# The product of w3 and w_out made in three chunks of 256 columns in place of two of 384

## The chip, the cores and the metric

One Trainium2 chip, one core. The metric is device time in microseconds of one execution. A difference is read from repeated runs of both kernels, taken side by side.

## What is computed

Attention over 4 batches of 12 heads with a soft cap, then four matrix products in a row on 1792 tokens:

```python
scores = cap * np.tanh(scale * q @ k.T / cap)
attn = softmax(scores)
x = (attn @ v)                      # laid out as 1792 x 768
a = x @ w1                          # 768 x 1024
b = x @ w2                          # 768 x 1024
h = a * b @ w3                      # w3: 1024 x 1024
out = h @ w_out                     # w_out: 1024 x 768
```

Weights are given as float64 and are split on the chip.

## The kernel before

The last two products are not made in the order of the reference. With u = a * b, the kernel makes C = w3 x w_out first (1024 x 768, it depends on no token) and then out = u x C. The second product is made by a scheme of Strassen's kind: seven products of quarter matrices, whose right operands are quarters of C and their differences.

The operands of these products are held as a high and a low part in fp32r. A product is three matmuls: high x high, high x low, low x high. Weights come as 64-bit floats: a *piece* of up to 384 columns is loaded as pairs of 32-bit words and turned into a high and a low part by a row of VectorE steps (lines 234, 246, 251, 254, 264, 271) and one or two ScalarE steps (239, and 268, the cast of the high part, which VectorE may also take).

The order on each engine is written out when the program is built, by a planner (`Plan.run`). Each step is a task with an engine (or two engines to choose from), a cost in ns, a key, and the tasks that it needs. The planner always takes the engine that is free first, and for it the ready task with the smallest key. What it emits is the fixed order of each engine's queue; on the chip each engine goes through its queue in that order, and waits on semaphores.

The stage that is changed is `plan_C(n)`, for n = 0 to 7. Each n makes one block of 128 rows of C: `it = ITS[n]` takes the rows in the order 0, 4, 1, 5, ..., so an upper block (`lower` = 0) is followed by the lower block with the same k. Before the change each n has two halves, nh = 0 and 1, of NH = 384 columns:

- 8 PE tasks (jt = 0 to 7, of three matmuls each, line 981) accumulate into one PSUM bank of the pool `ps_f`, which has six. The left operand is the w3 block (`w3t`, tile `w3x`, two buffers), the right one the rows `wo[jt]` of w_out. The three w3 pieces of a block cover jt = 0 to 2, 3 to 5 and 6 to 7 (`JG`). A task costs 521 in the plan. Its key is K0 + 40 + (n * 2 + nh) * 8 + jt.
- One copy (line 1006, task `D`) takes the bank to SBUF as `c`, 128 x 384, on ScalarE or VectorE, key K0.
- Then `split` makes the high part (line 1025, ScalarE or VectorE) and the low part (line 1029, VectorE) of that block, and `combine` (line 1050, VectorE) the differences; their keys, K0 - 1, come before those of the w3 pieces (K0 + 11.5 and up). The upper block gives B11 and T1, the lower one B21, B22, T2, T3 and T4.

After it come the output tasks (`plan_out`, line 1175, keys K0 + 200 and up): for each of seven t the seven products in the order 1, 5, 2, 3, 6, 7, 4, with 12 matmuls of 384 columns each. The first takes B11, the second T1, the third B21. The loads of `A` (line 1083) are issued on SP's queue, as the loads of the w3 pieces (line 227) are.

Of the kernel before, what the change touches and what calls it, by code (L numbers as in the profile page):

```python
# [8 lines left out]
F32 = mybir.dt.float32  # L9
# [139 lines left out]
def program(  # L149
# [16 lines left out]
    nc = tc.nc  # L166
    P = 128
    B, H, S, D = 4, 12, 448, 64
    NT, DM = out.shape
# [4 lines left out]
    KF = DF // P  # L174
    NH = DM // 2
    PC = 384
    KM = 384
    QO = 4
    CP, NCH = 112, 4
    SH = S // 2  # L180
# [23 lines left out]
    plan = Plan()  # L204
    plan.wait = {"PE": 32, "ACT": 119, "DVE": 91, "POOL": 0, "SP": 0}
    done, use = {}, {}

    def put(name, eng, ns, key, emit, needs=(), lat=0.0, alt=(), after=()):
        done[name] = plan.add(
            eng, ns, key, emit, [done.get(x) for x in needs], lat, alt, [done[x] for x in after]  # L210
        )
        done[name].name = name
        return done[name]
# [102 lines left out]
    KQ = 2 * S  # L316
    HK = KQ if general else S + KM
    att = ExitStack()
# [36 lines left out]
    def cuts(pr):  # L355

        return [slice(0, S + P), slice(S + P, HK)] if pr == 0 else [slice(0, HK)]

    def plan_load(pr):
        key = due(pr, 0) if pr % 2 else due(pr, 1)  # L360

        def emit():
            raw_t[pr] = qkp.tile([P, QO + KQ], F32, tag="raw", name=f"kq{pr}", bufs=3)
            for c in cuts(pr):
                c = slice(c.start + QO if c.start else 0, (c.stop if c.stop < HK else KQ) + QO)
                nc.sync.dma_start(raw_t[pr][:, c], kq[pr][:, c])
# [12 lines left out]
    def plan_split(pr):  # L379
# [3 lines left out]
        for n, c in enumerate(cuts(pr)):  # L383
            w = (c.stop - c.start) / HK

            def high(copy, n=n, c=c):
                if n == 0:
                    hl_t[pr] = qkp.tile([P, 2, HK], F32R, tag="hl", name=f"hl{pr}")
                copy(hl_t[pr][:, 0, c], raw_t[pr][:, QO + c.start : QO + c.stop])  # L389

            def low(c=c):
                h, l = (hl_t[pr][:, i, c] for i in range(2))
                nc.vector.tensor_tensor(
                    l, raw_t[pr][:, QO + c.start : QO + c.stop], h, op=ALU.subtract
                )
# [17 lines left out]
    def quarter(pr, j):  # L413

        j ^= pr % 2
        return slice(j * D, (j + 1) * D)

    def plan_S(pr, i):
# [5 lines left out]
        def scores():  # L424
            box[0] = ps_s.tile([P, 2, 512], F32, tag="s", name=f"s{pr}_{i}")
            if i == 0:
                for n in range(2):
                    for j in range(2):
                        at = slice(j * D, (j + 1) * D)
                        nc.tensor.matmul(  # L430
                            box[0][quarter(pr + n, j), n, :S],
                            lhsT=raw_t[pr + n][at, QO + S + KM :],
                            rhs=raw_t[pr + n][at, QO : QO + S],
                            start=True,
# [268 lines left out]
    def plan_general(pr):  # L703
# [3 lines left out]
        def emit():  # L707
# [4 lines left out]
            for c in range(NCH):  # L712
# [25 lines left out]
                for j in range(2):  # L738
# [5 lines left out]
                    for m, k1 in enumerate(ends):  # L744
                        k0 = m * P if m < 3 else KM - at.start
                        nc.tensor.transpose(
# [137 lines left out]
    NRAW, NRT, NOB, NF = 6, 3, 9, 6  # L884
    K0, CK = 500, 0.72
# [80 lines left out]
    bt, cf = {}, {}  # L966

    def plan_C(n):

        it = ITS[n]  # L970
        k, lower = it % HF, it // HF
        for nh in range(2):
            ns = slice(nh * NH, (nh + 1) * NH)
            box = {}
            for jt in range(KF):

                def emit(jt=jt, box=box, nh=nh, ns=ns):
                    if jt == 0:
                        box[0] = ps_f.tile([P, 512], F32, tag="f", name=f"pc{it}_{nh}")
                    for z, (a, c) in enumerate(((0, 0), (0, 1), (1, 0))):  # L980
                        nc.tensor.matmul(  # L981
                            box[0][:, :NH],
                            lhsT=w3t[n % 2][:, a, jt, :],
                            rhs=wo[jt][:, c, ns],
                            start=(jt == 0 and z == 0),
                            stop=(jt == KF - 1 and z == 2),
                        )

                key = K0 + 40 + (n * 2 + nh) * KF + jt
                z = [i for i, x in enumerate(JG) if x[0] <= jt < x[1]][0]  # L990
                t = put(
                    f"C{n}_{nh}_{jt}", "PE", 521, key, emit,
                    [f"O{jt}_{nh}high", f"O{jt}_{nh}out", f"Z{n}_{z}high", f"Z{n}_{z}out"]
                    + [f"C{n}_{nh}_{jt - 1}"],
                )
                if jt == 0:
                    f = plan.tag("f", NF).take(t)
                use["wo", jt // 2].append(t)
                for u in (use["w3t", n], use["w3y"]):
                    u.append(t)  # L1000

            c = f"c{lower}{nh}_{k}"

            def evac(cp, box=box, c=c):
                cf[c] = obp.tile([P, NH], F32, tag="ob", name=c)
                cp(cf[c], box[0][:, :NH])

            t = put(
                f"D{c}", "ACT", 400, K0, lambda f=evac: f(nc.scalar.copy), [f"C{n}_{nh}_{KF - 1}"],
                0, [("DVE", 450, lambda f=evac: f(nc.vector.tensor_copy))],  # L1010
            )
            f.append(t)
            t.key = key
            use[c] = plan.tag("ob", NOB).take(t)
            t.key = K0
            use[c].append(t)

        def split(name, c, after):


            def high(copy):
                if not bt:
                    for x in RHS.values():
                        bt[x] = big.tile([P, HF, 2, NH], F32R, tag="W", name=f"b{x}")
                copy(bt[name][:, k, 0], cf[c])

            def low():
                h, l = (bt[name][:, k, x] for x in range(2))
                nc.vector.tensor_tensor(l, cf[c], h, op=ALU.subtract)

            first = (name, k) == ("B11", 0)
            t = put(
                f"h{name}_{k}", "ACT", 412, K0 - 1, lambda: high(nc.scalar.copy),
                [after] + ["hB11_0"] * (not first), 0,
                [("DVE", 269, lambda: high(nc.vector.tensor_copy))],
            )
            use[c].append(t)
            if first:
                t.key = key
                for x in RHS.values():  # L1040
                    plan.tag("W", KF).take(t)
                t.key = K0 - 1
            t = put(f"l{name}_{k}", "DVE", 470, K0 - 1, low, [f"h{name}_{k}"])
            use[c].append(t)

        def combine(name, to, a, b, needs):


            def emit():
                nc.vector.tensor_tensor(cf[to], cf[a], cf[b], op=ALU.subtract)  # L1050

            t = put(name, "DVE", 470, K0 - 1, emit, needs)
            for x in {to, a, b}:
                use[x].append(t)

        c11, c12, c21, c22 = (f"c{x}_{k}" for x in ("00", "01", "10", "11"))
        if not lower:
            split("B11", c11, f"D{c11}")
            combine(f"T1_{k}", c11, c12, c11, [f"D{c12}", f"lB11_{k}"])
            split("T1", c11, f"T1_{k}")  # L1060
        else:
            split("B21", c21, f"D{c21}")
            split("B22", c22, f"D{c22}")
            combine(f"T3_{k}", c12, c22, c12, [f"D{c22}", f"T1_{k}"])
            combine(f"T2_{k}", c11, c22, c11, [f"D{c22}", f"lT1_{k}"])
            split("T2", c11, f"T2_{k}")
            split("T3", c12, f"T3_{k}")
            combine(f"T4_{k}", c21, c11, c21, [f"T2_{k}", f"lB21_{k}"])
            split("T4", c21, f"T4_{k}")
# [184 lines left out]
    with tc.manual_schedule():  # L1254
# [52 lines left out]
        ps_f = fin.enter_context(tc.tile_pool(name="ps_f", bufs=NF, space=PSUM))  # L1307
        wop = fin.enter_context(tc.tile_pool(name="wop", bufs=1))
        obp = fin.enter_context(tc.tile_pool(name="obp", bufs=NOB))
# [6 lines left out]
        for n in range(KF):  # L1316
            for z in range(len(JG)):
                plan_w3(n, z)
            plan_C(n)
# [75 lines left out]
```

## Time and profile before

| | us |
|---|---|
| median of 3 runs | 591.85 |
| lowest and highest | 590.34, 593.38 |
| span of the profiled execution | 589.8 |
| TensorE matmul busy | 571.9 (97%) |
| TensorE weight load busy | 448.6 (76%) |
| VectorE busy | 424.2 (72%) |
| ScalarE busy | 320.8 (54%) |

The span is the time from the first to the last instruction of one profiled execution; its own time outside the profile is not recorded, and the median of the runs is 2.05 us above the span. Busy time of matmuls is taken from modelled ends and overlaps from one matmul to the next, so the spacing of matmuls has to be worked out from a stretch and a count, not from the length of one. The page names instructions by the line of the program, the engine and the tiles: `pc<-wo,w3x` is the product that is changed, `pab` the products with w1 and w2 before it, `m` the output products after it, `c` the copied block, `bB` and `bT` its splits. In the rows PE is TensorE's matmul, PEld its weight load, DVE is VectorE and ACT ScalarE.

### The profile page before, as it was taken

How to read it: one execution, taken by the hardware profiler on the slowest of the kernel's cores; microseconds unless marked ns; L12 is line 12 of the kernel's file. 1: busy time of each engine (PE TensorE's matmuls, PEld its weight loads, DVE VectorE, ACT ScalarE, POOL GpSimd, SP SyncE). 2: the span in 40 equal slices, each digit the busy share in tenths (PEclk: the TensorE clock that was granted, in tenths of full speed). 3: DMA queues.
4: the chain of work that ended last, by engine and by line, in shares of the span. 5: the costliest groups of instructions: out<-in, count | busy, mean ns of one | idle time of the engine just before them, and what ended most of it. 6: DMA issues, size and time to landing. Idle time of an engine off the chain costs nothing.

```text
span 589.8 us, 8978 instructions
## 1 busy us (share of the span) xinstructions
PE 571.9 (97%) x3324; PEld 448.6 (76%) x3324; DVE 424.2 (72%) x910; ACT 320.8 (54%) x478; POOL 0.2 (0%) x4
## 2 busy tenths in 40 slices
PE   6989899999999999999999999999999999999995
PEld 3334386665588676667767779999999999999995
DVE  5999999899963536451726135999999998876611
ACT  7989857588833654645636412444455563443300
POOL 0000000000000000000000000000000000000000
PEclk9999999999999999999999999999999999999999
DMA  7355645554620303141212006555432225444111
GB/s 255 97 155 172 200 148 182 170 166 138 211 69 33 126 20 130 40 127 32 81 47 64 32 33 208 188 181 168 153 117 98 89 82 161 135 155 140 55 54 59
DMA packets 46517, 70.35 MB, mean 119 GB/s; under 512 B 5890, under 2 KB 34178, under 8 KB 46466
## 3 DMA queue, kind: packets, MB, share of 16 engines
q1 hardware_dynamic: 46466, 69.71, 37.2%
q8 instruction: 28, 0.46, 0.3%
q14 instruction: 23, 0.19, 0.1%
HBM read 56.67 MB, written 12.93 MB: 118 GB/s over the span
## 4 chain that ended last, share of the span: by engine, by line
PE 80%; DVE 12%; DMA 3%; ACT 2%; issue 1%; SPq 1%; DVEq 0%; ACTq 0%
PE pab L832 39%; PE m L1175 17%; PE pv L496 7%; PE pc L981 7%; PE s L443 6%; DMA raw_w<-in_moe_w_dram 2%; PE sum L573 2%; DVE t_w L246 1%; PE pv L511 1%; DVE raw_w L254 1%; PE s L430 1%; DVE a L559 1%; ACT p L456 1%; DVE raw_w L251 1%; DVE w3x L271 1%
## 5 line engine op out<-in xcount | busy, mean ns | idle before, releaser
L832 PE MATMUL pab<-x,w_hl 128*128 128x448 f32 x1152 | 248.7, 371 | 0.0
L832 PEld LDWEIGHTS pab<-x,w_hl 128*128 128x128 f32 x1152 | 212.6, 188 | 39.0 <-issue 11.0
L459 ACT ACTIVATE p<-p,ncap_sb,acap_sb 128x896 f32<-128x896 f32 x84 | 92.4, 1138 | 0.0
L456 ACT ACTIVATE p<-s,tsc_sb 128x896 f32<-128x896 f32 x84 | 81.5, 1012 | 18.3 <-PE s L443 16.5
L981 PE MATMUL pc<-wo,w3x 128*128 128x384 f32 x384 | 67.1, 335 | 1.1 <-DVE w3x L271 1.1
L981 PEld LDWEIGHTS pc<-wo,w3x 128*128 128x128 f32 x384 | 66.5, 188 | 1.6 <-DVE w3x L271 1.4
L443 PE MATMUL s<-hl 64*128 64x448 f32 x432 | 59.5, 397 | 7.2 <-ACT hl L389 4.4
L443 PEld LDWEIGHTS s<-hl 64*128 64x128 f32 x432 | 37.6, 190 | 35.3 <-issue 13.4
L496 PE MATMUL pv<-p,v 128*64 128x448 f32 x288 | 62.7, 554 | 1.2 <-DMA v<-in_v_dram 0.9
L559 DVE TENSOR_TENSOR a<-p,p 128x896 f32<-128x896 f32 x24 | 26.1, 1086 | 47.0 <-ACT xf L633 33.5
L1175 PE MATMUL m<-bB,lx 128*128 128x384 f32 x252 | 45.9, 334 | 0.0
L1175 PEld LDWEIGHTS m<-bB,lx 128*128 128x128 f32 x252 | 43.9, 188 | 0.0
L496 PEld LDWEIGHTS pv<-p,v 128*64 128x64 f32 x288 | 17.5, 137 | 31.8 <-issue 23.3
L239 ACT ACTIVATE t_w<-t_w,rebias 128x384 int32<-128x384 int32 (+1 forms) x48 | 28.4, 597 | 23.5 <-DVE t_w L234 23.2
L633 ACT COPY xf<-pv 128x448 f32<-128x448 f32 x24 | 12.8, 535 | 36.7 <-PE pv L496 18.4
L857 DVE TENSOR_TENSOR u<-pab,u 128x448 f32<-128x448 f32 x32 | 19.6, 613 | 18.3 <-PE pab L832 18.1
L1125 ACT CAST lx<-A 128x512 fp32r<-128x512 f32 x32 | 19.4, 620 | 23.7 <-DVE A L1101 9.2
L1175 PE MATMUL m<-bT,lx 128*128 128x384 f32 x168 | 31.4, 334 | 0.0
L246 DVE SCALAR_TENSOR_TENSOR t_w<-raw_w,t_w 128x384 int32<-128x384 int32 (+1 forms) x56 | 29.8, 534 | 2.0 <-ACT t_w L239 1.7
L1175 PE MATMUL m<-bT,lw 128*128 128x384 f32 x168 | 30.2, 334 | 0.0
L254 DVE SCALAR_TENSOR_TENSOR raw_w<-raw_w 128x384 f32<-128x384 uint32 (+1 forms) x56 | 29.8, 532 | 0.2
L1175 PEld LDWEIGHTS m<-bT,lx 128*128 128x128 f32 x168 | 29.3, 188 | 0.0
(81 smaller groups left out, 567.3 us busy)
## 6 DMA issues: line engine op xcount, KB each, us to landing
raw_w<-in_moe_w_dram SPq DMA_DIRECT2D x48, 384.0 KB
kq<-in_kq_dram SPq DMA_DIRECT2D x23, 450.0 KB
u_dr<-u SPq DMA_DIRECT2D x32, 224.0 KB
A<-u_dr SPq DMA_DIRECT2D x28, 256.0 KB
raw_wo<-in_moe_w_out_dram SPq DMA_DIRECT2D x16, 384.0 KB
v<-in_v_dram SPq DMA_DIRECT2D x24, 224.0 KB
r<-r_dr SPq DMA_DIRECT2D x48, 112.0 KB
out_dram<-o SPq DMA_DIRECT2D x14, 192.0 KB
```

The costliest lines, as they stand in the source:

```text
L239: nc.scalar.activation(self.t, self.t, AF.Relu, bias=rebias, scale=4096.0)
L246: nc.vector.scalar_tensor_tensor(self.t, self.hi, SIGN, self.t, op0=ALU.bitwise_and, op1=ALU.bitwise_or)
L254: nc.vector.scalar_tensor_tensor(self.lo.bitcast(F32), self.lo.bitcast(U32), 2.0**-32, self.hi, op0=ALU.mult, op1=ALU.add,)
L443: nc.tensor.matmul(box[0][:, j, :S], lhsT=hl[at, a, S + (i - 1) * P : S + i * P], rhs=hl[at, c, :S], start=(z == 0), stop=(z == 2),)
L456: nc.scalar.activation(p, box[0][:, :, :S], AF.Tanh, scale=tsc_sb)
L459: nc.scalar.activation(p_t[pr, i], p_t[pr, i], AF.Exp, scale=acap_sb, bias=ncap_sb)
L496: nc.tensor.matmul(pv_t[pr][j * D : (j + 1) * D, :S], lhsT=v_t[pr][:, 3 * j + i - 1, :], rhs=p_t[pr, i][:, j, :], start=(i == 1 and not od ...
L559: nc.vector.tensor_tensor(a_t[pr], p_t[pr, 1], p_t[pr, 2], op=ALU.add)
L832: nc.tensor.matmul(box[0][:, :S], lhsT=w_t[m][:, a, wi, kt, :], rhs=x_t[b][:, c, kt, :], start=(kt == 0 and z == 0), stop=(kt == KX - 1 an ...
L857: nc.vector.tensor_tensor(box[2][0], box[1][0][:, :S], box[2][0], op=ALU.mult)
L981: nc.tensor.matmul(box[0][:, :NH], lhsT=w3t[n % 2][:, a, jt, :], rhs=wo[jt][:, c, ns], start=(jt == 0 and z == 0), stop=(jt == KF - 1 and ...
L1175: nc.tensor.matmul(box[banks[m]][:, :NH], lhsT=hl[g][:, i, a, k, :], rhs=bt[RHS[m]][:, k, c, :], start=(new and k == 0 and z == 0), stop=( ...
```

## The change

Each block of C is made in three chunks of CW = 256 columns, and not in two halves of 384. A chunk is eight PE tasks of three matmuls of 256 columns into one bank. The first chunk lies in the first half of the output columns, the third in the second; the second chunk lies in both, so it is copied by two tasks of 128 columns, one into each half's tile `c`. The splits and differences still work on the 384 columns of a half and need both of its copies. The planned cost of a PE task goes from 521 to 333, that of a copy is set by its width, and the keys of the PE tasks are spread over the same stretch as before.

```diff
@@ -175,6 +175,7 @@
     NH = DM // 2
     PC = 384
     KM = 384
+    CW = 256
     QO = 4
     CP, NCH = 112, 4
     SH = S // 2
@@ -969,29 +970,30 @@
 
         it = ITS[n]
         k, lower = it % HF, it // HF
-        for nh in range(2):
-            ns = slice(nh * NH, (nh + 1) * NH)
+        for ch in range(DM // CW):
+            ns = slice(ch * CW, (ch + 1) * CW)
+            halves = range(ns.start // NH, (ns.stop - 1) // NH + 1)
             box = {}
             for jt in range(KF):
 
-                def emit(jt=jt, box=box, nh=nh, ns=ns):
+                def emit(jt=jt, box=box, ch=ch, ns=ns):
                     if jt == 0:
-                        box[0] = ps_f.tile([P, 512], F32, tag="f", name=f"pc{it}_{nh}")
+                        box[0] = ps_f.tile([P, 512], F32, tag="f", name=f"pc{it}_{ch}")
                     for z, (a, c) in enumerate(((0, 0), (0, 1), (1, 0))):
                         nc.tensor.matmul(
-                            box[0][:, :NH],
+                            box[0][:, :CW],
                             lhsT=w3t[n % 2][:, a, jt, :],
                             rhs=wo[jt][:, c, ns],
                             start=(jt == 0 and z == 0),
                             stop=(jt == KF - 1 and z == 2),
                         )
 
-                key = K0 + 40 + (n * 2 + nh) * KF + jt
+                key = K0 + 40 + n * 2 * KF + (ch * KF + jt) * CW / NH
                 z = [i for i, x in enumerate(JG) if x[0] <= jt < x[1]][0]
                 t = put(
-                    f"C{n}_{nh}_{jt}", "PE", 521, key, emit,
-                    [f"O{jt}_{nh}high", f"O{jt}_{nh}out", f"Z{n}_{z}high", f"Z{n}_{z}out"]
-                    + [f"C{n}_{nh}_{jt - 1}"],
+                    f"C{n}_{ch}_{jt}", "PE", 333, key, emit,
+                    [f"O{jt}_{nh}{x}" for nh in halves for x in ("high", "out")]
+                    + [f"Z{n}_{z}high", f"Z{n}_{z}out", f"C{n}_{ch}_{jt - 1}"],
                 )
                 if jt == 0:
                     f = plan.tag("f", NF).take(t)
@@ -999,21 +1001,29 @@
                 for u in (use["w3t", n], use["w3y"]):
                     u.append(t)
 
-            c = f"c{lower}{nh}_{k}"
-
-            def evac(cp, box=box, c=c):
-                cf[c] = obp.tile([P, NH], F32, tag="ob", name=c)
-                cp(cf[c], box[0][:, :NH])
-
-            t = put(
-                f"D{c}", "ACT", 400, K0, lambda f=evac: f(nc.scalar.copy), [f"C{n}_{nh}_{KF - 1}"],
-                0, [("DVE", 450, lambda f=evac: f(nc.vector.tensor_copy))],
-            )
-            f.append(t)
-            t.key = key
-            use[c] = plan.tag("ob", NOB).take(t)
-            t.key = K0
-            use[c].append(t)
+            for nh in halves:
+                c = f"c{lower}{nh}_{k}"
+                a, b = max(ns.start, nh * NH), min(ns.stop, (nh + 1) * NH)
+                first = a == nh * NH
+
+                def evac(cp, box=box, c=c, a=a, b=b, nh=nh, first=first, at=ns.start):
+                    if first:
+                        cf[c] = obp.tile([P, NH], F32, tag="ob", name=c)
+                    cp(cf[c][:, a - nh * NH : b - nh * NH], box[0][:, a - at : b - at])
+
+                w = (b - a) / NH
+                t = put(
+                    f"D{c}" if b == (nh + 1) * NH else f"D{c}a", "ACT", 140 + 260 * w, K0,
+                    lambda f=evac: f(nc.scalar.copy),
+                    [f"C{n}_{ch}_{KF - 1}"] + [f"D{c}a"] * (not first),
+                    0, [("DVE", 60 + 390 * w, lambda f=evac: f(nc.vector.tensor_copy))],
+                )
+                f.append(t)
+                if first:
+                    t.key = key
+                    use[c] = plan.tag("ob", NOB).take(t)
+                    t.key = K0
+                use[c].append(t)
 
         def split(name, c, after):
```

## Rows read from the trace of the kernel before

**Rows 1.** The page: span, busy (share, instructions), clock, chain, `pab` group.

```profile
span 589.8 us, 8978 instructions
...
PE 571.9 (97%) x3324; PEld 448.6 (76%) x3324; DVE 424.2 (72%) x910; ACT 320.8 (54%) x478; POOL 0.2 (0%) x4
...
PEclk9999999999999999999999999999999999999999
...
PE 80%; DVE 12%; DMA 3%; ACT 2%; issue 1%; SPq 1%; DVEq 0%; ACTq 0%
...
L832 PE MATMUL pab<-x,w_hl 128*128 128x448 f32 x1152 | 248.7, 371 | 0.0
```

**Rows 2.** Chain that ended last, in order of time: start, length, what.

```profile
399.85 13.64 PE pab L832 x66
413.49 24.81 PE pc L981 x143
438.30 0.02 issue
438.32 0.42 DVE w3x L271
438.74 0.47 DVE c L1006
...
467.49 0.48 DVE w3x L271
467.97 0.04 issue
468.01 13.58 PE pc L981 x76
481.59 101.94 PE m L1175 x588
```

**Rows 3.** Instructions in order of time: start, length, what, idle before.

```profile
413.33 12.99 PE L981 MATMUL pc<-wo,w3x 128*128 128x384 f32 x74
...
468.01 13.27 PEld L981 LDWEIGHTS pc<-wo,w3x 128*128 128x128 f32 x76 [1.44 <-DVE w3x L271]
468.01 13.58 PE L981 MATMUL pc<-wo,w3x 128*128 128x384 f32 x76 [1.12 <-DVE w3x L271]
...
481.43 2.24 PE L1175 MATMUL m<-bB,lx 128*128 128x384 f32 x12
```

**Rows 4.** Waits of TensorE's matmuls from 400 us: total, times, longest.

```profile
PE pc L981 <- DVE w3x L271: 1.1, 1, 1.1
```

**Rows 5.** Windows: length, busy us of each engine (instructions), clock, DMA.

```profile
438.30:468.00 29.70, 28.59 (x165) 28.27 (x164) 29.67 (x81) 16.23 (x33) 0.00 (x0) 1.00 0.32 102
...
490.00:500.00 10.00, 10.00 (x60) 10.00 (x59) 8.22 (x15) 3.00 (x6) 0.00 (x0) 1.00 0.63 190
```

**Rows 6.** Chain in order of time, an earlier stretch of `pab`.

```profile
166.63 17.21 PE pab L832 x84
```

**Rows 7.** In order of time: two weight loads after the stall, second's matmul.

```profile
468.01 0.19 PEld L981 LDWEIGHTS pc<-wo,w3x 128*128 128x128 f32 x1 [1.44 <-DVE w3x L271]
...
468.12 0.19 PEld L981 LDWEIGHTS pc<-wo,w3x 128*128 128x128 f32 x1
...
468.29 0.52 PE L981 MATMUL pc<-wo,w3x 128*128 128x384 f32 x2
```

**Rows 8.** In order of time: copies of the sixth block's two halves.

```profile
461.84 0.46 ACT L1006 COPY c<-pc 128x384 f32<-128x384 f32 x1
...
463.45 0.48 ACT L1006 COPY c<-pc 128x384 f32<-128x384 f32 x1
```

**Rows 9.** Line 1006, the copies: ns min/median/max, first and last start.

```profile
L1006 ACT COPY c<-pc x12: 459/482/482, 421.9 to 481.6; 128x384 f32<-128x384 f32 x12
L1006 DVE COPY c<-pc x4: 549/552/558, 417.7 to 455.3; 128x384 f32<-128x384 f32 x4
```

**Rows 10.** Groups by form, 413 to 482 us: busy, mean ns, idle.

```profile
L268 ACT CAST w3x<-t_w 128x384 fp32r<-128x384 f32 x12 | 6.2, 514 | 9.0 <-DVE t_w L246 9.0
...
L268 ACT CAST w3x<-t_w 128x256 fp32r<-128x256 f32 x7 | 2.8, 407 | 2.6 <-DVE t_w L246 2.6
...
L271 DVE SCALAR_TENSOR_TENSOR w3x<-raw_w 128x384 fp32r<-128x384 f32 x14 | 7.7, 548 | 0.0
...
L271 DVE SCALAR_TENSOR_TENSOR w3x<-raw_w 128x256 fp32r<-128x256 f32 x8 | 3.3, 415 | 0.0
```

**Rows 11.** Tile `c`, a row of low parts: ns, first and last start.

```profile
L1029 DVE TENSOR_TENSOR bT<-c,bT x16: 540/546/554, 423.8 to 486.0; 128x384 fp32r<-128x384 f32 x16
```

## The prediction, made before the changed kernel was run

> **What bounds the kernel now.** I read the page first. TensorE matmul is busy 97% of a span of 589.8 us, VectorE 72%, ScalarE 54%, the granted clock is full throughout (the 2.4 GHz level), and the chain that ended last is 80% TensorE and 12% VectorE [rows 1]. Averages don't say which of the two holds the stage that is changed, so I took the chain in order of time next [rows 2]. It runs on TensorE through the last `pab` matmuls and 143 matmuls of `pc`, leaves TensorE at 438.30 us, goes through VectorE without a break until 467.97 us (467.49 + 0.48), and comes back to TensorE for the last 76 `pc` matmuls. Then 588 output matmuls run for 101.94 us with nothing between them. So the product w3 x w_out, from 413.33 us (first `pc` matmul [rows 3]) to 481.43 us (first output matmul, same rows), 68.10 us in all, is held by TensorE at both ends and by VectorE in the middle.
>
> The matmul view of that stage shows one stall: TensorE waits before 468.01 us for the low part of a w3 piece, and the weight loader shows 1.44 us idle for it [rows 3]. It is the only wait of TensorE after 400 us [rows 4]. The windows agree: from 438.30 to 468.00 us VectorE is busy 29.67 of 29.70 us, ScalarE 16.23 [rows 5]. The reader is to see two things: VectorE has no slack in the stage, and TensorE has about 1.5 us of it. 384 matmuls at 173.4 ns (below) are 66.59 us of the 68.10, so 1.51 us are stall.
>
> The median of the three runs is 591.85 us, 2.05 above the profiled span of 589.8; I keep that distance and add my difference in span to the median.
>
> **The matmuls.** Removed are 8 x 2 x 24 = 384 matmuls of 384 columns, added 8 x 3 x 24 = 576 of 256. The columns are the same (147,456); the weight loads go up by half. Before, one matmul takes 173.4 ns: 101.94 us / 588 in the output stage and 24.81 / 143 = 173.5 in `pc` [rows 2]. At 2.4 GHz 384 columns are 160.0 ns, so 13.4 ns are on top. The `pab` matmuls with 448 columns (186.7 ns) take 13.64 / 66 = 206.7 ns right before the stage [rows 2], 20.0 on top, and in an earlier stretch (17.21 - 0.37) / 83 = 202.9 ns, 16.2 on top, taking the length of the last one off, 371 ns [rows 1, 6]. No 256-column matmul with 128-column weights is in this trace, so its price is bounded from these rows. Streaming alone is 106.7 ns.
> - Lowest: the surplus shrinks with the columns (the line through 384 and 448 gives 106.8), and the weight load is the floor. After the stall, two weight loads of this shape start at 468.01 and 468.12 us [rows 7], so the loader needs about 110 ns for one: 110.
> - Proportional: 173.4 x 256/384 = 115.6.
> - A fixed 13.4 on top: 120.1. The 20.0 of the 448-column row on top: 126.7.
>
> I take 115.6: 384 is the nearest width, and 202.9 / 448 and 173.4 / 384 are 0.453 and 0.452 ns per column, so one of the two 448-column rows lies on that line. The planner counts 333 ns for three, 111 each; that is a number of the diff and not of a trace.
>
> By the warm rule of the Trainium skill (TensorE: Matmul & The Clock Gate, Back-to-back issue gap), columns / 2.4 plus 2.5 ns, a 256-column matmul would take 109.2 ns, and 576 of them 62.9 us. The same rule gives 162.5 ns for 384 columns where the row shows 173.4, so the trace does not agree and my value doesn't rest on it.
>
> **What of it reaches the end.** TensorE arrives at the stall after 308 of the 384 matmuls. The 308 are 462 narrow ones, 53.4 us at 115.6, the same arrival as before, and VectorE is not ready until 467.97 anyway. The waited-for piece isn't needed earlier: the planner lets TensorE run whatever triple is ready, and it did. The first-half and second-half copies of one w3 column block start at 461.84 and 463.45 us, 1.6 us apart [rows 8], where 24 matmuls are 4.16 us, so both halves were run side by side up to the missing piece. Three chunks can do the same, with the same number of columns free of it. After the stall 76 x 1.5 = 114 matmuls are left, 13.18 us at 115.6, where 481.43 - 468.01 = 13.42 us stand now (76 x 173.4 = 13.18 and 0.24 for starting up). That is no change. At 110 the rest is 0.64 us shorter, and a faster TensorE before 468 us only waits longer. At 120.1 TensorE would arrive at 413.33 + 462 x 0.1201 = 468.8, after VectorE: the stall is gone and 576 x 0.1201 = 69.18 us stand against 68.10, +1.08.
>
> **The copies out of PSUM.** Removed are 16 copies of 384 columns, added 32: per w3 block 256, 128, 128 and 256, since the middle chunk lies in both halves of the output columns. Before, ScalarE made 12 (median 482 ns) and VectorE 4 (552) [rows 9]. For the narrow ones I go by forms in this stage: ScalarE's cast is 514 ns for 384 and 407 for 256, VectorE's last step 548 and 415 [rows 10]. That is 0.84 and 1.04 ns per column, so ScalarE copies take about 375 and 268 ns, 2 x 643 = 1286 per block in place of 964. Eight blocks cost ScalarE 2.6 us more, covered by 13.5 idle us in the middle stretch alone [rows 5]. On VectorE there is no cover. There one copy takes 0.47 us of the chain [rows 2], and by the same slope about 0.34 and 0.20 for 256 and 128. If a quarter stays on VectorE, as now, that is 8 x 0.27 = 2.2 us for 4 x 0.47 = 1.9. Ends: none on VectorE, -1.9 us; half of them, 16 x 0.27 = 4.3, +2.4. I take +0.4, a little above a quarter, because the middle chunk makes two copies ready at once and ScalarE can start only one.
>
> **Edits that I cost at nothing.** The first half's block is complete at two thirds of its time, not at half, so its high/low splits and subtractions wait 1.4 us longer (a sixth of the 48 x 173.4 ns of a block). VectorE has w3 pieces to do meanwhile; without them it would idle those 1.4 us. At the end, the second operand of the output stage is first needed after 24 of its matmuls, 481.43 + 4.16 = 485.6 us. Its copy, cast and subtraction are about 0.37 + 0.51 + 0.55 us after the middle chunk's end; if that cover went, the output stage would wait the remainder. The last splits of the stage start at 486.0 us now [rows 11], and VectorE falls to 8.22 of 10 us busy after 490 [rows 5]. PSUM banks: 24 groups take turns in 6 banks, three open per block, and no wait for a bank is in the waits [rows 4]; one would cost a copy, about 0.4 us. On the SP queue the w3 loads and the loads of `A` queue behind one another; they are released by VectorE's piece steps, so they move with VectorE's chain, and no output matmul waited for one.
>
> **Sum.** Matmuls 0, copies +0.4 us: 591.85 + 0.4 = 592.3 us.
>
> **The rivals.**
> 1. Narrow matmuls at the floor and VectorE relieved. TensorE takes 110 ns (-0.64) and ScalarE makes all the copies (-1.9): -2.5 us, 589.3. For it: ScalarE is idle almost half the stretch. Against it: the planner gave VectorE a quarter with the same idle time there. Chance 0.12.
> 2. Slower: each weight load costs the matmul stream a fixed 20 ns, as in the 448-column row. 576 x 126.7 = 72.98 us against 68.10: +4.9, 596.7. It decides from (68.10 + 2.95) / 576 = 123.3 ns per matmul on, where the stall's 1.5 us are used up and 0.5% is passed. For it: half as many more weight loads, and one row with that surplus. Against it: the nearer width shows 13.4. Chance 0.15.
> 3. Slower by order. The planner counts 111 ns, and its order is fixed. If a matmul really takes 120, TensorE falls behind by 24 x 27 ns = 0.65 us per block, 3.9 us by the sixth. A copy put into VectorE's queue then waits for TensorE with the w3 steps queued behind it, and these feed TensorE. With three of those 3.9 us lost in VectorE's chain the time is about 595.3. Chance 0.12.
> 4. The weight path sets the period. After the stall a load starts at 468.12 us and its matmul at 468.29, 0.17 us later [rows 7]; if a load and its matmul always take that long and only one load can run ahead, 576 x 173.4 = 99.9 us, +31.8, 623.7. Against it: at 448 columns that limit would be hidden, leaving 187 to 190 ns where 203 to 207 stand, and two loads were 110 ns apart. Chance 0.04. The same page of the Trainium skill says under "What overlaps and what doesn't" that a weight load overlaps a running matmul only in another row group; 160 + 110 ns for every matmul would follow, and 173.4 in the row speaks against it.
>
> **How the numbers follow.** The forecast, VectorE holding the end of the stage within some 1.5 us of today, gets 0.57: 592.3 us. The range runs from 589.3 (rival 1) to 596.7 (rival 2); beyond it lie rival 4 and the tails of 1 and 3, about 0.17. A difference of 0.5%, 2.95 us, is about what a measurement of this kernel can tell from no change. Faster by more needs rival 1 and something on top: 0.08. Slower by more is rival 2, rival 4, and part of rival 3: 0.26. The rest, 0.66, is within 0.5%.
>
> **What would show it.** Of the profile after: the mean spacing of `pc` matmuls (115.6 against 110, 120 and 127); the number of copies on VectorE (about 9 of 32); a chain that still leaves TensorE for VectorE until about 468 us and one wait of TensorE for a w3 piece; the first output matmul at about 481.8 us; 588 output matmuls still in 102 us. A spacing of 123 ns or more, a wait of VectorE for a `pc` matmul over a microsecond, or a first output matmul before 479 us would make the forecast wrong.

## The result, and the profile after

The changed kernel takes 597.27 us (median of nine runs, 595.98 to 599.16) where nine runs of the kernel before beside it give 592.92. The ratio is 1.0084, with a 95% interval of 1.0067 to 1.0101: slower, by 5.0 us going by the ratio (the two medians lie 4.35 us apart). My 592.3 us stood for no difference that can be measured.

The profiled execution has a span of 596.9 us, 7.0 more than before. I split it by the same three points in both traces. The first `pc` matmul comes 1.75 us later (415.08 against 413.33). The order of TensorE's matmuls up to there is the same in both kernels, and most of the delay arises around 75 us, where the granted clock was 0.60 over 4 us (1.00 before) and matmuls of `pab` came 374 ns apart. That belongs to the execution and not to the change: over all fourteen traces, with the same order before it, the first `pc` matmul starts anywhere from 412.77 to 416.99 us. From the first `pc` matmul to the end of the last output matmul it takes 175.24 us against 170.18, **+5.06**. What follows takes 0.2 us more. The +5.06 is the difference that the times show, and I compare all runs below by this stretch.

Windows (length, busy us of TensorE's matmuls, weight loads, VectorE, ScalarE and GpSimd with instructions, clock, DMA). First the stretch around 75 us before the change:

```profile
73.00:77.00 4.00, 4.00 (x19) 2.23 (x16) 3.97 (x12) 4.00 (x6) 0.00 (x0) 1.00 0.33 106
```

Then the same stretch and the product stage after it:

```profile
73.00:77.00 4.00, 4.00 (x14) 2.04 (x10) 2.96 (x9) 4.00 (x6) 0.00 (x0) 0.60 0.34 101
...
415.08:488.22 73.14, 70.05 (x577) 69.31 (x576) 70.61 (x193) 33.28 (x74) 0.00 (x0) 1.00 0.31 99
```

The stage is 73.14 us where 68.10 stood, and VectorE, which had no idle time to speak of before [rows 5], is idle for 2.53 us of it. The chain that ended last, in order of time (start, length, what), answers [rows 2]:

```profile
415.24 32.41 PE pc L983 x270
...
447.67 0.28 ACT c L1012
...
454.27 0.48 DVE w3x L272
...
454.79 11.91 PE pc L983 x97
...
473.80 4.36 PE pc L983 x34
...
479.56 8.83 PE pc L983 x70
488.39 101.94 PE m L1185 x588
```

Before, it left TensorE once, for VectorE. Now it leaves three times, each time through a copy of `c` on ScalarE and then on VectorE, the splits and other steps behind it, and a w3 step. 32.41 us / 270 are 120.0 ns per matmul. The 588 output matmuls take the 101.94 us of before.

The waits of VectorE in the stage (total us, times, longest), and the copies (ns min/median/max, first and last start), which answer [rows 9]:

```profile
DVE c L1012 <- ACT c L1012: 1.5, 4, 0.5
DVE c L1012 <- PE pc L983: 0.6, 3, 0.2
```
```profile
L1012 ACT COPY c<-pc x18: 266/319/377, 421.0 to 487.9; 128x128 f32<-128x128 f32 x9, 128x256 f32<-128x256 f32 x9
L1012 DVE COPY c<-pc x14: 291/356/425, 418.2 to 488.5; 128x256 f32<-128x256 f32 x7, 128x128 f32<-128x128 f32 x7
```

VectorE makes 14 copies, not 4, and each of these waits, 2.1 of its 2.53 idle us, stands in front of a copy: for the matmul, or for ScalarE's copy out of the same bank. The second of the three stalls in order of time:

```profile
466.72 0.27 ACT L1012 COPY c<-pc 128x128 f32<-128x128 f32 x1 [0.35 <-PE pc L983]
467.02 0.29 DVE L1012 COPY c<-pc 128x128 f32<-128x128 f32 x1 [0.46 <-ACT c L1012]
...
469.64 0.55 DVE L1060 TENSOR_TENSOR c<-c,c 128x384 f32<-128x384 f32 x1
...
472.73 0.55 DVE L1039 TENSOR_TENSOR bT<-c,bT 128x384 fp32r<-128x384 f32 x1
473.19 0.55 DVE L272 SCALAR_TENSOR_TENSOR w3x<-raw_w 128x384 fp32r<-128x384 f32 x1
...
473.80 0.74 PE L983 MATMUL pc<-wo,w3x 128*128 128x256 f32 x4 [1.47 <-DVE w3x L272]
```

The matmul ends, ScalarE copies 128 columns of the middle chunk, VectorE has idled 0.46 us for that and copies the other 128. Its splits, differences and steps of other w3 pieces follow, and only behind them the w3 step that TensorE has been standing for. Of the 0.46 us, 0.30 are ScalarE's half going first (466.72 to 467.02). The plan lists no need between the two halves of the middle chunk (the diff above shows the needs), so it doesn't count that wait; a plan that has it was not tried.

### The profile page after: what moved, and what is told of

It reads as the page before. It is cut to its first block, busy times and chain, and to the rows that moved or that the text cites. A ratio compares the mean times of both kernels' runs of the same rounds, so it can differ in the third digit from the quotient of the medians.

```text
span 596.9 us, 9364 instructions
## 1 busy us (share of the span) xinstructions
PE 576.6 (97%) x3516; PEld 452.1 (76%) x3516; DVE 431.1 (72%) x929; ACT 317.3 (53%) x475; POOL 0.2 (0%) x4
## 4 chain that ended last, share of the span: by engine, by line
PE 83%; DVE 9%; DMA 3%; ACT 2%; issue 1%; SPq 1%; DVEq 0%; ACTq 0%
PE pab L833 39%; PE m L1185 17%; PE pc L983 10%; PE pv L497 7%; PE s L444 6%; DMA raw_w<-in_moe_w_dram 2%; PE sum L574 2%; PE pv L512 1%; ACT p L457 1%; PE s L431 1%; DVE a L560 1%; DVE t_w L247 1%; DMA kq<-in_kq_dram 1%; ACT p L460 1%; DVE raw_w L255 1%
## 5 line engine op out<-in xcount | busy, mean ns | idle before, releaser
L983 PE MATMUL pc<-wo,w3x 128*128 128x256 f32 x576 | 70.2, 284 | 3.1 <-DVE w3x L272 3.0
L983 PEld LDWEIGHTS pc<-wo,w3x 128*128 128x128 f32 x576 | 69.5, 192 | 3.9 <-DVE w3x L272 3.7
```

Source lines behind the costliest of these rows:

```text
L983: nc.tensor.matmul(box[0][:, :CW], lhsT=w3t[n % 2][:, a, jt, :], rhs=wo[jt][:, c, ns], start=(jt == 0 and z == 0), stop=(jt == KF - 1 and ...
```

## The experiments

Two theories after the result. **Order:** the planner counts 333 ns for three matmuls, they take 360. It places copies and splits in the queues too early, and VectorE waits in front of them with w3 steps behind. **Load:** 14 copies on VectorE are more work than 4, and VectorE was full. Beside both, the **matmul's surplus**: 576 x 120.0 = 69.12 us in place of 66.56.

The stretch from the first `pc` matmul to the end of the last output matmul, taken from the records of each trace, with the idle time of VectorE (gaps over 50 ns) up to the last `pc` matmul. "Copies on VectorE" are those of `c`:

| kernel | plan ns | copies on VectorE | stretch us | against before | VectorE idle us | ratio of times (95%) |
|---|---|---|---|---|---|---|
| before | 521 | 4 of 16 | 170.18 | | 0.2 | |
| changed | 333 | 14 of 32 | 175.24 | +5.06 | 2.5 | 1.0084 (1.0067 to 1.0101) |
| e1 | 360 | 13 of 32 | 171.58 | +1.40 | 0.1 | 1.0028 (1.0013 to 1.0043) |
| e2, e11 | 333 | 0 of 32 | 172.63 | +2.45 | 2.4 | 1.0038, 1.0031 |
| e12 | 336 | 0 of 32 | 171.20 | +1.02 | 2.3 | 1.0014 (0.9999 to 1.0029) |
| e3 | 360 | 0 of 32 | 171.20 | +1.02 | 0.1 | 1.0009 (0.9995 to 1.0023) |
| e9 | 347 | 12 of 32 | 173.05 | +2.87 | 1.5 | 1.0038 (1.0024 to 1.0052) |
| e10 | 390 | 12 of 32 | 174.52 | +4.34 | 0.1 | 1.0092 (1.0070 to 1.0115) |
| e4 (384 columns) | 521 | 10 of 32 | 170.48 | +0.30 | 0.1 | 1.0000 (0.9980 to 1.0021) |
| e5 (384 columns) | 521 | 0 of 16 | 168.78 | -1.40 | 0.3 | 0.9981 (0.9965 to 0.9996) |
| e6 (384 columns) | 482 | 5 of 16 | 171.24 | +1.06 | 2.1 | 1.0018 (1.0003 to 1.0034) |

The kernel of e2 and e11 does not compute the product: its output is off by about a tenth, the same both times, and which step of its order does that stays open. Its times are of the same number of matmuls and copies as those of e3 and e12, but no part of the account below rests on them alone.

**e1: the plan's number put right.**

```diff
-                    f"C{n}_{ch}_{jt}", "PE", 333, key, emit,
+                    f"C{n}_{ch}_{jt}", "PE", 360, key, emit,
```

> The changed kernel with one number altered: the planner counts 360 ns for three matmuls of 256 columns (what the trace of the changed kernel shows, 3 x 120.0) in place of 333. The product stage (first pc matmul to first output matmul) is 68.10 us before and 73.15 us after; 576 x 120.0 = 69.12 us of that is matmul spacing. Theory order (copies put too early into VectorE's queue, 2.48 us of VectorE idle in front of them, w3 steps queued behind): the idle time falls under 0.5 us and the stage to about 70.7 us, time about 1.004 of before. Rival load (14 copies on VectorE in place of 4, and the order is innocent): the stage stays within 0.7 us of 73.15 and the time at about 1.008.

Measured: VectorE's idle time is gone, the stretch falls by 3.66 us to +1.40. The load is nearly the same: of the steps that either engine may take, VectorE makes 13 copies and 13 casts (lines 269 and 1035) where the changed kernel has 14 and 13, 0.7 us less in sum. No instruction was added or altered; the order is another, and with it which engine makes a few of the steps. The order theory holds: it had given the stage about 2.5 us back, and the stretch got 3.66. The copies by duration:

```profile
L1012 ACT COPY c<-pc x19: 262/363/377, 420.2 to 483.8; 128x256 f32<-128x256 f32 x10, 128x128 f32<-128x128 f32 x9
L1012 DVE COPY c<-pc x13: 274/292/424, 417.3 to 484.8; 128x128 f32<-128x128 f32 x7, 128x256 f32<-128x256 f32 x6
```

**e2: all copies on ScalarE, 333 kept.**

```diff
-                    0, [("DVE", 60 + 390 * w, lambda f=evac: f(nc.vector.tensor_copy))],
+                    0, (),
```

> The changed kernel with all 32 copies out of PSUM on ScalarE; the planner still counts 333. Theory order: VectorE's queue no longer holds a copy, so no copy can wait there, but its splits still wait for ScalarE's copies, at the same points of the plan; VectorE idle stays above 1.5 us and the stage above 72 us. Rival load: VectorE is relieved of 14 copies (5.0 us busy) and the stage falls to about 70 us, time about 1.003 of before.

Measured: VectorE still idles 2.4 us, now in front of the splits, as the order theory said. But the stretch fell to +2.45, which is nearer to what the load theory had said. Neither had the whole of it.

**e3: both edits.**

> Both edits: 360 ns in the plan and all 32 copies on ScalarE. If the stage is 576 matmuls at 120.0 ns plus stalls that order and load make, both are taken away here: stage 69.1 to 70.0 us, VectorE idle under 0.5 us, time 1.002 to 1.004 of before. Theory that a stall is left because of something else (the w3 pieces come late whatever the copies do): stage over 71 us.

Measured: no stall at all, and a ratio of 1.0009, under the 1.002 that I had expected at least. Chain in order of time:

```profile
413.43 69.11 PE pc L983 x576
482.55 101.94 PE m L1185 x588
```

69.11 / 576 = 120.0 ns. What is left against before, +1.02, is the surplus of 192 more matmuls (2.56 us) less the stall of 1.5 us that the kernel before has and this one does not.

**e4: the copies alone**, on the kernel before.

```diff
-            def evac(cp, box=box, c=c):
-                cf[c] = obp.tile([P, NH], F32, tag="ob", name=c)
-                cp(cf[c], box[0][:, :NH])
+            for a, b in ((0, 256), (256, NH)) if nh == 0 else ((0, 128), (128, NH)):
+                ...
+                    cp(cf[c][:, a:b], box[0][:, a:b])
```

> The kernel before, with its 384 matmuls of 384 columns, and only the copies cut: each half's bank is copied as 256 + 128 (first half) or 128 + 256 (second half) columns, 32 copies in all with the costs of the changed kernel. Theory that the copies' own load is what stalls the stage: stage 70 us or more, time 1.003 or more. Theory that the matmul's surplus and the plan that miscounts it make the loss: stage 68.1 to 69.0 us, time within 0.2% of before.

Measured: +0.30 us in the stretch, ratio 1.0000. Cutting 16 copies into 32, 10 of them on VectorE, costs next to nothing where the plan counts the matmuls right.

**e5: the kernel before with its copies on ScalarE.**

```diff
-                0, [("DVE", 450, lambda f=evac: f(nc.vector.tensor_copy))],
+                0, (),
```

> The kernel before with its 16 copies of 384 columns all on ScalarE (4 were on VectorE). Theory that the load of copies on VectorE matters little by itself (0.4 us between the two runs of the 256-column kernel with 360 ns in the plan): time within 0.25% of before, 1.5 us of stall at most to be gained. Rival load theory: VectorE's four copies are what keeps the w3 piece back, the stall of 1.5 us goes, ratio 0.997 to 0.998.

Measured: ratio 0.9981 (0.9965 to 0.9996). By itself that fits both theories, since the first allowed 0.25%; what decides is the stall. Chain, and the copies:

```profile
412.93 66.70 PE pc L981 x384
479.62 101.94 PE m L1175 x588
```
```profile
L1006 ACT COPY c<-pc x16: 460/482/482, 417.1 to 479.7; 128x384 f32<-128x384 f32 x16
```

The stall of [rows 3] is gone: 66.70 us are 384 x 173.7. With the four copies off VectorE no w3 step comes late, as the rival had it. This kernel is the fastest of all, by 0.2% against before.

**e6: the miscount alone**, on the kernel before: 482 in place of 521.

> The kernel before with one number altered: the planner counts 482 ns for three matmuls of 384 columns in place of 521, as far below the trace (3 x 173.4 = 520) as 333 is below 360. No matmul and no copy is changed. Order theory: the miscount alone costs; VectorE idles in front of copies for 1 to 3 us, from the first pc matmul to the last output matmul it takes 171.5 to 174 us (170.2 before), ratio 1.002 to 1.006. Rival (a miscount costs only together with narrow matmuls and 32 copies): ratio within 0.1% of 1.

Measured: +1.06 us, ratio 1.0018 (1.0003 to 1.0034), both just under what the order theory had given. The ratio's interval does not rule out the rival's 0.1%; the stretch and the idle time speak against it, since VectorE idles 2.1 us, within the theory's 1 to 3. Its waits and those of TensorE:

```profile
DVE c L1006 <- PE pc L981: 0.9, 2, 0.5
DVE bB L1029 <- ACT bB L1025: 0.7, 2, 0.5
DVE bB L1025 <- ACT c L1006: 0.6, 2, 0.4
```
```profile
PE pc L981 <- DVE w3x L271: 2.0, 2, 1.3
```

A miscount of the same 7.5% costs something without narrow matmuls too, but only a third of what e1 gave back.

**e7: 192 columns, the matmul's price at a smaller width.** Four chunks, 280 in the plan.

```diff
-    CW = 256
+    CUTS = (0, 192, 384, 576, 768)
...
-                    f"C{n}_{ch}_{jt}", "PE", 333, key, emit,
+                    f"C{n}_{ch}_{jt}", "PE", 3 * (cw / 2.4 + 13.4), key, emit,
```

> The changed kernel with four chunks of 192 columns (768 matmuls, 32 copies of 192 columns, none across the halves), and 280 ns in the plan for three matmuls (3 x (80.0 + 13.4)). Fixed surplus: 80.0 + 13.4 = 93.4 ns each, 71.7 us of matmuls, ratio about 1.008 with some stall. Weight load as the floor: two loads never stand closer than 108 ns in the traces, so 108 to 110 ns each, 83 to 84 us, ratio 1.022 to 1.03.

```profile
413.04 85.74 PE pc L984 x768
498.78 101.25 PE m L1186 x584
```

85.74 / 768 = 111.6 ns, without a stall of TensorE. The fixed surplus would be 93.3. Single matmuls start 110 to 115 ns apart, and in none of the traces do two weight loads of this shape start less than 107 ns apart; so the weight load is what fits as the bound at 192 columns, and 256 with its 120.0 lies just above it. That it is the load, and not another floor of the matmul, was not shown apart. The ratio is 1.0284 (1.0262 to 1.0306).

**e8: 512 and 256 columns**, `CUTS = (0, 512, 768)`, the plan's cost as in e7.

> Chunks of 512 and 256 columns: 384 matmuls as before, 24 copies (384, 128, 256), and the plan counts 3 x (columns / 2.4 + 13.4). Fixed surplus of 13.3 ns: 226.7 ns for 512 columns, 120.0 for 256, 66.6 us of matmuls as before, time within 0.25% of before. Surplus that grows above 384 columns, as 448 columns with 16 to 20 ns suggest: 235 to 245 ns for 512, 68 to 70 us of matmuls, ratio up to 1.004.

Measured: most 512-column matmuls start 226 or 227 ns apart, 13.3 over 213.3, some 228 to 236; the 256-column ones 120. The busy time by form (mean ns behind it is that of one, with its pipeline):

```profile
L984 PE MATMUL pc<-wo,w3x 128*128 128x512 f32 x192 | 46.3, 393 | 1.3 <-DVE w3x L272 1.3
L984 PE MATMUL pc<-wo,w3x 128*128 128x256 f32 x192 | 24.7, 282 | 0.0
```

The ratio is 1.0014 (1.0000 to 1.0028), the stretch +0.77, with TensorE again waiting for w3 steps (2.3 us in all). Fewer chunks of unequal width bring nothing. The plan's numbers were close to the measured ones here, and TensorE stalls more than before the change (1.5 us): a right number alone does not take the stall away.

**e9: half the miscount, 347**, which is 3 x 115.6, my own forecast's value.

> The changed kernel with 347 ns in the plan (3 x 115.6, the value of my forecast), half way between 333 (+5.1 us from the first pc matmul to the last output matmul, against the kernel before) and 360 (+1.4). Theory that the loss grows with the miscount (13 ns x 24 tasks x 8 blocks = 2.5 us of drift in place of 5.2): +2 to +4 us, ratio 1.004 to 1.007, VectorE idle 0.5 to 2 us in front of copies. Rival (the one order made with 333 is unlucky, and the size of the miscount says nothing): within 0.5 us of the run with 360, or as slow as 333.

Measured: +2.87, ratio 1.0038, a little under the range of the ratio that I had given, VectorE idle 1.5 us, all in front of copies. With 333, 347 and 360 the stretch goes 175.24, 173.05, 171.58: in these three orders the loss grows with the miscount. How far a close neighbour of 333 with copies on both engines would scatter was not tried.

**e10: the plan's number too high, 390.**

> The changed kernel with 390 ns in the plan, 30 above what the trace shows. If only a count that is too low harms (copies placed before their matmuls end), VectorE has no idle time in front of copies here, copies come late and the PSUM banks take the difference: within 0.7 us of the run with 360, ratio 1.002 to 1.004. If any miscount harms: +3 us or more, ratio 1.005 or more.

Measured: +4.34 us, ratio 1.0092. The theory that only a low count harms falls. VectorE does not idle here (0.1 us). Instead steps of the output stage stand in its queue ahead of the last w3 step, while TensorE waits:

```profile
477.53 0.69 DVE L1139 TENSOR_TENSOR lx<-A,lx 128x512 fp32r<-128x512 f32 x1
...
479.60 0.69 DVE L1111 TENSOR_TENSOR S<-A,A 128x512 f32<-128x512 f32 x1
480.20 0.42 DVE L272 SCALAR_TENSOR_TENSOR w3x<-raw_w 128x256 fp32r<-128x256 f32 x1
...
480.68 6.50 PE L983 MATMUL pc<-wo,w3x 128*128 128x256 f32 x52 [1.88 <-DVE w3x L272]
```

Those two steps hold the queue for 1.2 us (0.60 each, start to start) of the 2.9 that e10 loses against e1, which has about the same copies. How the rest comes about was not followed further and stays open.

**e11: e2 once more.**

> The run with all copies on ScalarE and 333 ns in the plan once more: same stretch as there, 172.6 us from the first pc matmul to the last output matmul within 0.3 us, ratio 1.0025 to 1.005. With it, 360 against 333 is worth 1.4 us where no copy is in VectorE's queue and 3.7 us where 14 are.

Measured: 172.63 us again, ratio 1.0031 (1.0014 to 1.0049).

**e12: 336 with all copies on ScalarE.**

> The changed kernel with 336 ns in the plan (24 too low where 333 is 27 too low) and all copies on ScalarE: a neighbouring order with no copy in VectorE's queue. Theory that a miscount costs less where VectorE holds no copy: 171.8 to 173.2 us from the first pc matmul to the last output matmul (171.2 with 360 and copies on ScalarE, 175.2 in the changed kernel), VectorE idle 1 to 2.5 us, ratio 1.002 to 1.005. Rival (the miscount costs its 3.7 us whoever copies): over 174.5 us, ratio over 1.006.

Measured: 171.20 us, as with 360, and a ratio of 1.0014, both under what I had expected (171.8 us and 1.002 at least). TensorE does not stall, though VectorE idles 2.3 us. Chain in order of time:

```profile
417.15 63.71 PE pc L983 x531
480.87 1.56 PE m L1185 x9
482.43 5.39 PE pc L983 x45
487.82 100.38 PE m L1185 x579
```

The waits of VectorE in e2's order (e11's trace) show in front of what it idles when it makes no copies:

```profile
DVE bB L1035 <- ACT c L1012: 1.5, 5, 0.4
DVE c L1060 <- ACT c L1012: 0.5, 1, 0.5
```

**What follows.** VectorE has a budget in this stage. The miscount takes about 2.4 us of it as idle time, 14 copies take 5.0 us busy. With the idle time alone (e12) TensorE is not held up at all, in the neighbouring order of e2 by 1.4 us; but e2 also has 16 casts on VectorE where e12 has 10. With the copies alone (e1) it is 0.4 us. With both it is 4.0 us (175.24 - 171.20). The two don't add up as separate terms on TensorE. On VectorE they nearly do, as the last start of the w3 step that TensorE waits for shows, in the order e3, e12, e1, changed:

```profile
L272 DVE SCALAR_TENSOR_TENSOR w3x<-raw_w x24: 405/545/552, 409.3 to 477.3; 128x384 fp32r<-128x384 f32 x16, 128x256 fp32r<-128x256 f32 x8
L272 DVE SCALAR_TENSOR_TENSOR w3x<-raw_w x24: 416/550/557, 413.0 to 483.2; 128x384 fp32r<-128x384 f32 x16, 128x256 fp32r<-128x256 f32 x8
L272 DVE SCALAR_TENSOR_TENSOR w3x<-raw_w x24: 409/545/553, 410.3 to 481.8; 128x384 fp32r<-128x384 f32 x16, 128x256 fp32r<-128x256 f32 x8
L272 DVE SCALAR_TENSOR_TENSOR w3x<-raw_w x24: 416/551/557, 411.1 to 485.4; 128x384 fp32r<-128x384 f32 x16, 128x256 fp32r<-128x256 f32 x8
```

Their first `pc` matmuls start at 413.27, 416.99, 414.27 and 415.08 us, so the last w3 step starts 64.0, 66.2, 67.5 and 70.3 us behind them: 2.2 us later by the miscount (336 there), 3.5 by the copies, 6.3 by both. TensorE stands 0, 0, 0.4 and 4.0 us for it. The loss appears where the sum goes past the slack. Taken off one after the other, the +5.06 are these: 1.02 is the matmul's surplus net of the old stall, 0.38 are the copies on VectorE in a right order (e1 - e3), and 3.66 is the order made with 333 (changed - e1). That 3.66 is the price of the order with these copies on VectorE, and not of the number by itself.

## Why the prediction was wrong, point by point

- *What bounds the stage.* Right: VectorE full, TensorE with 1.5 us of stall. e5 shows it from the other side.
- *The matmul's price.* I took 115.6 between 110 and 126.7; it is 120.0, the fixed surplus that I had listed with 13.4. I had taken the proportional value because one 448-column row lay on that line. The three widths that now stand beside it (256, 384 and mostly 512) have 13.3 on top; the 448-column rows with 16 to 20 are the odd ones. My own text gave +1.08 for 120.1, and e3 measures +1.02, stall gone, as written there. As a term it was 1.0 us too small, and not the cause of the miss.
- *The copies.* I counted 9 on VectorE and +0.4 us; there were 14. In a right order they cost 0.38 (e1 - e3), and cut alone on the kernel before 0.30 (e4). That this is the size of my term is luck: at my prices the 13 copies of e1 are 3.4 us of VectorE (7 x 0.20 + 6 x 0.34), its last w3 step does start 3.5 us later than in e3, and TensorE had slack for all but 0.38 of it. I had not seen that the middle chunk's two copies follow one another: VectorE's half waits for ScalarE's, four times, 1.5 us in all by the waits above.
- *The edits costed at nothing.* The step that failed is "VectorE has w3 pieces to do meanwhile". That would hold for a queue that picks its next step while it runs. This one is written out beforehand, with the matmuls at 111 ns each, so VectorE stands in front of the copy with the w3 pieces behind it. It idles 2.5 us there, TensorE stands 4.0 us for w3 steps in place of 1.5, and the right number in the plan gives 3.66 us back (e1). I had written this down as rival 3 and given it 0.12.
- *Rival 3.* Its mechanism is what the runs show, and its size was nearly right: 3.0 us priced, 3.66 measured. But I added it to 592.3, a sum for 115.6 ns, though it needs matmuls of 120 ns, which carry 1.08 us themselves. With them it would have read 596.4, against 596.8 (591.85 x 1.0084). And its chance was too low: 120 was one of the values that I held possible, and at every such value but the lowest, 110, the plan was off.
- *Rival 1.* Did not come: the price was not at the floor. *Rival 2*: 123.3 ns was not reached; that the time came out near its 596.7 is chance, the cause is another. *Rival 4*: ruled out, 120.0 ns and not 173.4.
- *Signs.* The output matmuls held (588 in 101.94 us). The first of them came at 488.22 us and not at about 481.8, and the chain left TensorE for a w3 piece three times and not once. "A wait of VectorE for a `pc` matmul over a microsecond" was the sign against the forecast; it did not show, since VectorE's waits are 0.6 us in all for the matmul itself and 1.5 for ScalarE's copy behind it.

## What to carry to other kernels

Where a queue's order is written out with assumed costs, a change of an operation's size is two changes: the operation's own price, and every step placed by its assumed price. Check the assumed number against the nearest rows first; here, with 12 to 14 copies on the full VectorE, a number 7.5% too low cost 3.7 us and one 8% too high 2.9, where the operation itself cost 1.0. With no copy there, one 7% too low cost nothing (e12). And where the engine beside the bound is full, look at what could be taken off it before reshaping the bound's work: moving four copies from VectorE to ScalarE was worth more (-0.2%) than any width of matmul tried.

## What the runs showed of the hardware

- A matmul with a 128 x 128 weight load in front of it starts 13.3 ns later than its columns take at 2.4 GHz, at 256 columns (120.0), 384 (173.3) and for the most part 512 (226.7). I had expected the surplus to go with the columns. The Trainium skill (TensorE: Matmul & The Clock Gate, Back-to-back issue gap) gives, for an isolated matmul, a warm gap of columns / 2.4 plus a fixed 2.5 ns. That the surplus is fixed agrees with these three widths; its size, in these streams of weight loads and matmuls, does not.
- At 192 columns it is 111.6 ns, not 93.3, in a stream of 768 matmuls. The weight load fits as the bound there (no two of this shape start less than 107 ns apart in any trace); it was not shown apart from other causes.
- Two copies out of one PSUM bank, one by ScalarE and one by VectorE, followed one another in the changed kernel: where ScalarE went first, VectorE's copy started 0.30 us behind it (466.72 and 467.02). The trace shows it released by ScalarE's copy; whether both could read the bank at once was not tried.
